# Merging the two strip tasks of V into one task of the scheduler

## The chip, the cores and the metric

The kernel runs on one core of a Trainium2 chip. The metric is the device time of one execution in microseconds (us). Times are medians of several runs; a ratio is the mean time of one kernel's fast runs over the mean of the other's in the same rounds, so it is not quite the ratio of the medians quoted beside it. The kernel before has a median of 1903.02 us (1902.42 to 1903.92, three runs).

## The reference, cut to what matters

Two layers A alternate with two feed-forward layers B. Layer A walks over the sequence in 64 segments of 32 rows; 8 rows of memory, made from the attention output of one segment, go into the next. So the steps form a chain.

```python
def _A_ref(x, mem0, Wq, Wk, Wv, Wo, seg_len):      # Wq, Wk, Wv: 512 x 32 heads x 128
    mem = mem0
    for s in range(n_seg):                         # 64 segments
        h = jnp.concatenate([mem, x[:, s*seg_len:(s+1)*seg_len, :]], axis=1)     # 40 rows
        q, k, v = (jnp.einsum('btd,dhe->bhte', h, W) for W in (Wq, Wk, Wv))
        scores = jnp.where(mask, jnp.einsum('bhqe,bhke->bhqk', q, k) * scale, -1e9)
        o = jnp.einsum('bhqk,bhke->bhqe', softmax(scores), v)
        o = jnp.einsum('bhte,hed->btd', o, Wo)
        mem = o[:, :M, :]                          # feeds the next segment
        outs.append(o[:, M:, :])
# x = x + A(layernorm(x)); x = x + B(layernorm(x)); and both once more
```

The four layers are pipelined: step t computes segment t of the first layer A and segment t - 6 of the second, 70 steps in all, with layers B as filler.

## The kernel before

The kernel is recorded as tasks. A planner (a list scheduler with 24 rounds, made in Python before anything runs) gives each task an engine, a place in that engine's order, and its buffers. A task on TensorE is never interrupted, but two tasks can be separated by any other that is more urgent. L568 and the like are lines of the kernel. PSUM is the memory into which the kernel's matmuls write, in the eight banks of its pool `bank`; the tiles `qku`, `ptsb`, `otsb` and `sst` hold copies out of it.

```python
class Kern:
    ...
        self.bank = Pool([... 8 PSUM banks ...], {"bg": 3, "v": 3})
    ...
    def emit_step(self, t):
        ...
        vb = [pl.buf(self.bank), pl.buf(self.bank)]

        def strips(q):
            for c in range(DC):                    # 4 chunks of the contraction
                for i in range(4):                 # 4 strips of 32 partitions
                    k = 2 * i + q
                    nc.tensor.matmul(vb[q][32 * i:32 * i + 32, :], lhsT=hT[:, c, SCOL:SCOL + 32], rhs=self.wv[:, c, k * 512:(k + 1) * 512],
                                     start=(c == 0), stop=(c == DC - 1), skip_group_check=True)

        def add_strips():
            sb = pl.buf(self.sstp)
            for q in range(2):
                pl.add("PE", DC * (mm_ns(512) + 12) + 75, lambda q=q: strips(q), r=hkeys + [("wv", h) for h in range(H)], w=[vb[q]], use=[sb])
            for q in range(2):
                pl.add(("ACT", "DVE"), copy_ns(512), lambda q=q: (sb[:, q, :], vb[q][:, :]), r=[vb[q]], w=[(sb, q)], use=[sb])
            for i in range(4):
                vu = (4 * t + i) % 5
                pl.add("SP", 430, ...)             # transfer of sb into rows 32 to 63 of the V tile
        ...                                        # q and k (L704), scores (L718), softmax, transposes (L777)
                                                   # P V (L788), output projection (L805)
```

The V rows of the x part are computed in advance for whole blocks (L568). The 32 rows that hold the fresh memory can be computed only in the step itself: these are the strips. A strip matmul has only 32 output partitions, and four run side by side: in the trace of the kernel before they start 2 to 4 ns apart, and the next four 206 ns later in the median. 2 x 16 matmuls fill two PSUM banks. A visit to the strips, below, is a run of strip matmuls with nothing else of TensorE between them. By mode is meant here the output's width: 32 partitions in a strip, and 40, 80 or 128 in the matmuls next to the strips. A switch is the step in TensorE's order from the one to the other. The copies into `sst` and the transfer into the V tile `vsb` follow; P V waits for that tile.

## Time and profile before

| | before |
|---|---|
| median of the timed runs | 1903.02 us |
| profiled run | 1906.87 us |
| TensorE busy | 1853.5 us, 97% |
| waits of TensorE, summed over its view | 44.3 us |
| visits to the strips in TensorE's order | 113 (27 of 32 matmuls, 86 of 16) |
| strip copies on ScalarE and VectorE | 131 and 9 |

How to read it: TensorE is nearly always busy, so what counts is how it spends its busy time. The end that the profile gives for a matmul is modelled, and can lie after the next one's start (904.60 + 1.05 = 905.65 against 905.58 in the prediction's second timeline); the start of the next group less the start of this one, the slot, is what a group really takes of the engine. The prediction below shows the lines. Waits are idle times of more than 0.15 us. The profiled run was 3.9 us slower than the median. The granted clock, used further below, is the share of TensorE's full clock that the chip let it have, as the profile records it (0.992 in the profiled run before).

### The profile page before, as it was taken

What the parts mean: (1) busy time and instruction counts of PE and PEld (TensorE: products, weight loads), DVE (VectorE), ACT (ScalarE), POOL (GpSimd) and SP (SyncE); (2) the same over time, 40 slices, a digit from 0 to 9 for tenths busy, and PEclk for the clock granted to TensorE, in tenths of its full rate; (3) what the DMA queues carried; (4) which work ended last, traced back from release to release, by engine and by line L of the source; (5) the groups of instructions that cost most, each with busy time, mean ns of one, the idle gap of its engine ahead of it and who ended that gap; (6) DMA issues with size and microseconds to landing.
All of it is one profiled execution on the core that took longest, in us unless ns stands there. A gap on an engine that the chain in (4) does not pass through costs nothing.

```text
span 1905.1 us, 94394 instructions
## 1 busy us (share of the span) xinstructions
PE 1853.5 (97%) x41250; PEld 1579.6 (83%) x41250; DVE 1284.5 (67%) x4214; ACT 1192.4 (63%) x2722; POOL 580.1 (30%) x824
## 2 busy tenths in 40 slices
PE   7999899999999999989999999999999999999998
PEld 3578788988988888979888888988888898988786
DVE  5456577776777667756766777767776677766664
ACT  5655567666666666656665666666666666666554
POOL 5412012332424142332413232232413232333311
PEclk9999999999999999999999999999999999999999
DMA  9733324554635454544635454464635444454534
GB/s 350 243 92 106 86 61 141 149 155 118 185 106 165 116 168 127 155 138 128 179 84 172 120 155 140 128 178 134 174 97 167 128 137 141 134 161 138 161 94 139
DMA packets 133965, 273.84 MB, mean 144 GB/s; under 512 B 29254, under 2 KB 65358, under 8 KB 133550
## 3 DMA queue, kind: packets, MB, share of 16 engines
q0 software_dynamic: 59104, 181.61, 32.7%
q1 hardware_dynamic: 74446, 86.19, 15.7%
q8 instruction: 323, 5.29, 1.2%
q14 instruction: 92, 0.75, 0.1%
HBM read 222.04 MB, written 27.26 MB: 131 GB/s over the span
## 4 chain that ended last, share of the span: by engine, by line
PE 87%; DMA 4%; DVE 4%; issue 2%; ACT 2%; SPq 1%; POOL 1%; ACTq 0%; POOLq 0%; DVEq 0%
PE bank L704 30%; PE bank L805 15%; PE bank L904 10%; PE bank L568 8%; PE bank L674 6%; PE bank L928 5%; PE bank L718 5%; PE bank L788 4%; PE bank L777 3%; DMA vsb<-sst 2%; PE bank L538 1%; DMA scr<-vst 1%; DMA xo<-in_A_x_dram 1%; SPq L685 1%; DVE st L731 0%
## 5 line engine op out<-in xcount | busy, mean ns | idle before, releaser
L704 PE MATMUL bank<-hT,wq_sb 128*128 128x80 bf16 (+1 forms) x8960 | 624.8, 198 | 2.8 <-DVE hT L823 0.8
L704 PE MATMUL bank<-hT,wk_sb 128*128 128x80 bf16 (+1 forms) x8960 | 623.4, 198 | 0.4 <-issue 0.4
L996 ACT CAST qku<-bank 128x480 bf16<-128x480 f32 (+3 forms) x770 | 394.6, 512 | 259.3 <-PE bank L704 233.4
L704 PEld LDWEIGHTS <-wq_sb 128*128 128x128 bf16 x8960 | 458.5, 99 | 30.0 <-issue 10.0
L704 PEld LDWEIGHTS <-wk_sb 128*128 128x128 bf16 x8960 | 451.2, 99 | 1.3 <-issue 1.3
L731 DVE TENSOR_TENSOR st<-bank,maskb 80x240 f32<-80x240 f32 (+1 forms) x732 | 269.5, 369 | 196.0 <-PE bank L718 187.3
L805 PE MATMUL bank<-otsb,wo_sb 128*128 128x80 bf16 (+1 forms) x8960 | 375.7, 199 | 3.5 <-ACT otsb L996 2.7
L805 PEld LDWEIGHTS <-wo_sb 128*128 128x128 bf16 x8960 | 341.9, 100 | 14.2 <-issue 4.6
L896 POOL DMA_DIRECT2D wg<-in_B_w_gate_dram x217 | 164.4, 757 | 479.4 <-PE bank L904 430.1
L996 ACT CAST otsb<-bank 128x480 bf16<-128x480 f32 (+3 forms) x420 | 198.7, 486 | 106.2 <-PE bank L788 75.1
L922 POOL DMA_DIRECT2D wd<-in_B_w_down_dram x217 | 154.0, 711 | 221.1 <-PE bank L928 171.2
L526 POOL TENSOR_TENSOR lns<-lns,negh 128x1 f32<-128x1 f32 (+1 forms) x79 | 49.0, 621 | 531.0 <-DVE lns L525 430.1
L760 DVE TENSOR_TENSOR pb<-st,rz 80x480 bf16<-80x480 f32 x348 | 206.0, 593 | 4.4
L743 DVE TENSOR_REDUCE sm<-st 80x6 f32<-80x240 f32 (+3 forms) x420 | 152.8, 364 | 71.7 <-ACT st L741 69.6
L741 ACT ACTIVATE st<-st 80x240 f32<-80x240 f32 (+3 forms) x420 | 159.9, 381 | 27.5 <-DVE st L738 24.5
L718 PE MATMUL bank<-qku 128*80 128x80 bf16 (+1 forms) x2240 | 173.6, 203 | 1.3 <-ACT qku L996 0.3
L718 PEld LDWEIGHTS <-qku 128*80 128x80 bf16 (+1 forms) x2240 | 128.3, 117 | 55.4 <-ACT qku L996 17.0
L904 PE MATMUL bank<-xnT,wu 128*128 128x128 bf16 (+2 forms) x1784 | 171.3, 218 | 1.3 <-DMA wu<-in_B_w_up_dram 1.3
L904 PE MATMUL bank<-xnT,wg 128*128 128x128 bf16 (+2 forms) x1784 | 172.1, 219 | 0.0
L996 ACT CAST ptsb<-bank 128x480 bf16<-128x480 f32 (+3 forms) x277 | 134.5, 495 | 50.9 <-PE bank L777 46.8
L788 PE MATMUL bank<-ptsb,vsb 128*128 128x80 bf16 (+1 forms) x2240 | 141.7, 199 | 24.2 <-DMA vsb<-sst 10.4
L897 POOL DMA_DIRECT2D wu<-in_B_w_up_dram x217 | 163.0, 751 | 5.3 <-PE bank L904 1.6
(103 smaller groups left out, 2578.0 us busy)
## 6 DMA issues: line engine op xcount, KB each, us to landing
wg<-in_B_w_gate_dram POOLq DMA_DIRECT2D x219, 256.0 KB, 4.3
wd<-in_B_w_down_dram POOLq DMA_DIRECT2D x219, 256.0 KB, 4.8
wu<-in_B_w_up_dram POOLq DMA_DIRECT2D x218, 256.0 KB, 4.9
vsb<-scr SPq DMA_DIRECT2D x512, 48.0 KB
vsb<-sst SPq DMA_DIRECT2D x280, 64.0 KB
scr<-vst SPq DMA_DIRECT2D x128, 96.0 KB
wv_sb<-in_A_Wv_dram SPq DMA_DIRECT2D x4, 1024.0 KB
wq_sb<-in_A_Wq_dram SPq DMA_DIRECT2D x5, 768.0 KB
```

The source lines that it names most:

```text
L704: nc.tensor.matmul(o_ap, lhsT=W[:, c, h * P:(h + 1) * P], rhs=mv(c), start=(c == 0), stop=(c == DC - 1))
L718: nc.tensor.matmul(s_all(SB)[pr, uh - h0 + i, :], lhsT=qku[:, i, 0, 0:ncol], rhs=qku[:, i, 1, 0:ncol], start=True, stop=True)
L731: pl.add("DVE", dve_ns(n, True), lambda gsz=gsz, hs=hs, st=st, SB=SB, pj_=pj_, npj_=npj_, mk=mk, idx=idx: nc.vector.tensor_tensor(out=st[p ...
L741: pl.add("ACT", act_ns(n), lambda hs=hs, st=st: nc.scalar.activation(out=st[pr, hs], in_=st[pr, hs], func=ACTF.Exp, scale=self.scale), r=s ...
L760: nc.vector.tensor_tensor(out=o, in0=st[pr, hs].unsqueeze(1).to_broadcast([npart, 2, gsz, L]), in1=rz[pr, :, 0:gsz].unsqueeze(3).to_broadc ...
L788: nc.tensor.matmul(OB[:, hl * ncol:(hl + 1) * ncol], lhsT=self.vsb[(4 * t + h // 8) % 5][:, (h % 8) * P:(h % 8 + 1) * P], rhs=ptsb[:, hl, ...
L805: nc.tensor.matmul(WB[:, c * ncol:(c + 1) * ncol], lhsT=self.wo[:, h, c * P:(c + 1) * P], rhs=otsb[:, hl, 0:ncol], start=(h == 0 and c == ...
L896: pl.add("POOL", 760, lambda wg=wg, fs=fs: nc.gpsimd.dma_start(out=wg[:], in_=self.wgv[:, :, fs]), r=[("wo", self.H - 1)], w=[gk] + bt, la ...
L897: pl.add("POOL", 760, lambda wu=wu, fs=fs: nc.gpsimd.dma_start(out=wu[:], in_=self.wuv[:, :, fs]), r=[("wo", self.H - 1)], w=[uk] + bt, la ...
L904: nc.tensor.matmul(gu[:, 2 * i + k, 0:n], lhsT=W[:, c, i * P:(i + 1) * P], rhs=xnT[:, c, rw], start=(c == 0), stop=(c == DC - 1))
L922: pl.add("POOL", 760, lambda wd=wd, ip=ip: nc.gpsimd.dma_start(out=wd[:], in_=self.wdv[:, 2 * ip:2 * ip + 2, :]), w=[dk] + (["boot"] if se ...
L996: nc.scalar.copy(out=dst, in_=src)
```

## The change

The intent, as it was described, is one task of eight concurrent streams in place of two tasks of four. The loop over the banks moves into the task. The order of the 32 matmuls in it is as before.

```diff
-        def strips(q):
-            for c in range(DC):
-                for i in range(4):
-                    k = 2 * i + q
-                    nc.tensor.matmul(vb[q][32 * i:32 * i + 32, :], ...)
+        def strips():
+            for q in range(2):
+                for c in range(DC):
+                    for i in range(4):
+                        k = 2 * i + q
+                        nc.tensor.matmul(vb[q][32 * i:32 * i + 32, :], ...)
 
         def add_strips():
             sb = pl.buf(self.sstp)
-            for q in range(2):
-                pl.add("PE", DC * (mm_ns(512) + 12) + 75, lambda q=q: strips(q), r=..., w=[vb[q]], use=[sb])
+            pl.add("PE", 2 * DC * (mm_ns(512) + 12) + 150, strips, r=..., w=vb, use=[sb])
```

More of the change, by code (lines that the diff above doesn't have):

```diff
@@ L668, in emit_step @@
         vb = [pl.buf(self.bank), pl.buf(self.bank)]
-        def strips(q):
-            for c in range(DC):
-                for i in range(4):
-                    k = 2 * i + q
-                    nc.tensor.matmul(vb[q][32 * i:32 * i + 32, :], lhsT=hT[:, c, SCOL:SCOL + 32], rhs=self.wv[:, c, k * 512:(k + 1) * 512],
-                                     start=(c == 0), stop=(c == DC - 1), skip_group_check=True)
+        def strips():
[3 more added lines that the diff above has]
+                        k = 2 * i + q
+                        nc.tensor.matmul(vb[q][32 * i:32 * i + 32, :], lhsT=hT[:, c, SCOL:SCOL + 32], rhs=self.wv[:, c, k * 512:(k + 1) * 512],
+                                         start=(c == 0), stop=(c == DC - 1), skip_group_check=True)
         def add_strips():
             sb = pl.buf(self.sstp)
-            for q in range(2):
-                pl.add("PE", DC * (mm_ns(512) + 12) + 75, lambda q=q: strips(q), r=hkeys + [("wv", h) for h in range(H)], w=[vb[q]], use=[sb])
+            pl.add("PE", 2 * DC * (mm_ns(512) + 12) + 150, strips, r=hkeys + [("wv", h) for h in range(H)], w=vb, use=[sb])
             for q in range(2):
```

## The prediction

> **What bounds the kernel now.** I read the share of busy time first, then the chain that ended last, then what the TensorE waits for, then the order of single groups on it.
>
> ```profile
> span 1905.1 us, 94394 instructions
> PE 1853.5 (97%) x41250; PEld 1579.6 (83%) x41250; DVE 1284.5 (67%) x4214; ACT 1192.4 (63%) x2722; POOL 580.1 (30%) x824
> PE 87%; DMA 4%; DVE 4%; issue 2%; ACT 2%; SPq 1%; POOL 1%; ACTq 0%; POOLq 0%; DVEq 0%
> L674 PE MATMUL bank<-wv_sb,hT 128*32 128x512 bf16 x2240 | 141.6, 381 | 0.0
> ```
>
> TensorE is busy 97% of the span and holds 87% of the chain that ended last; the vector and scalar engines have a third of their time free. So a change counts here by what it does to TensorE's own queue. The strips of V, the subject of the change, are the 2240 matmuls of the last line: 70 steps of 32. They show no idle time before them. Two lines of the wait view tell where TensorE does stand still: 10.4 us for the transfer that carries the strips into the V tile, and 7.7 us for one kind of copy.
>
> ```profile
> PE bank L788 <- DMA vsb<-sst: 10.4, 14, 2.1
> PE bank L788 <- DVE ptsb L998: 7.7, 5, 5.7
> ```
>
> All waits of that list add up to about 44 us, most of them at the start, where loads are outstanding, and at the end. The middle is dense: between 300 and 1800 us the table by stretches gives TensorE 1480.6 us busy of 1500.
>
> But "busy" hides something, because ends of matmuls are modelled. I therefore compare starts: the slot of a group is the next group's start minus its own. Here is TensorE's timeline in two steps, one in which the two strip tasks stand together and one in which they are apart:
>
> ```profile
> 557.31 0.31 PE L704 MATMUL bank<-hT,wk_sb 128*128 128x80 bf16 x4
> 557.55 1.91 PE L674 MATMUL bank<-wv_sb,hT 128*32 128x512 bf16 x32
> 559.39 0.42 PE L718 MATMUL bank<-qku 128*80 128x80 bf16 x6
> ```
>
> ```profile
> 904.16 0.51 PE L718 MATMUL bank<-qku 128*80 128x80 bf16 x9
> 904.60 1.05 PE L674 MATMUL bank<-wv_sb,hT 128*32 128x512 bf16 x16
> 905.58 0.31 PE L718 MATMUL bank<-qku 128*80 128x80 bf16 x3
> 905.82 1.05 PE L674 MATMUL bank<-wv_sb,hT 128*32 128x512 bf16 x16
> 906.79 0.32 PE L704 MATMUL bank<-hT,wq_sb 128*128 128x80 bf16 x4
> ```
>
> Together: 32 matmuls hold the engine 559.39 - 557.55 = 1.84 us. Apart: 0.98 and 0.97, so 1.95 for the same 32. The 16 by themselves should stream four deep in 4 x 0.216 = 0.86, the rate of the ordinary 512-wide matmuls (L568, 8 in 1.72 us): each visit to the strips pays about 0.115 us on leaving. It also pays on entering: four L704 matmuls take 0.143 us each time, but 0.24 ahead of the strips (+0.10); three L718 matmuls take 0.11 elsewhere and 0.24 ahead of the second half (+0.13). Over the whole trace, the median excess is 117 ns in the groups that follow strips out, and 97 (after L704), 113 (after L718) and 99 ns (after L928) in the groups ahead of them.
>
> [...] the changed loop also keeps its two banks one after the other. The trace agrees: 32 strips take 1.84 us, twice 0.86 plus one switch. The array's work does not shrink.
> [...]
>
> **The change part by part.**
>
> It removes no matmul, weight load or byte: TensorE has 41251 matmuls in both built programs, and the loop inside the new task is in the old order (bank, contraction chunk, strip). What changes is that the scheduler can no longer put another task between the two halves. The order of the built programs says how much that is: before, the strips form 113 visits (27 of 32 matmuls, 86 of 16), so 43 of the 70 steps are split, by anything from 3 short matmuls to 140. After, there are 70 visits, all of 32.
>
> So 43 entries and 43 exits go. The entries before stand behind L704 45 times (0.097), L718 43 times (0.113), L928 20 times (0.099): about 0.105 each. Sum: 43 x (0.105 + 0.117) = **9.5 us**. Check by the pair of steps above: apart 1.95 + 0.13 for the second entry against 1.84, which is 0.24 a step. All of it lies on TensorE, in the dense middle of the kernel, so nearly all of it should be on the path: 9.5 us or 0.5% of 1903.
>
> What moves: the copies out of the banks become due together. Before, ScalarE does 131 of the 140 and VectorE 9; in the changed order 82 and 58. Some ptsb copies go the other way (ScalarE 277 to 295), so VectorE gains 13 instructions net: 13 x 0.69 (its strip copy) = 9 us on an engine with over 600 us free. Nothing on the path.
>
> What it adds: each task needs both banks at once and holds the first one some 0.9 us longer, and a score matmul (L718) that comes due just after the strips began waits up to 1.84 us instead of 0.98. In the split steps the second half now comes earlier. From the order, weighing each matmul by its streaming time and each switch by 0.11 us, I estimate the work on TensorE between the last strip and the first use of the V tile: under 6 us in 66 of 70 steps before, in 53 after. The transfer behind the 10.4 us of waits thus has a little more room.
>
> **The rivals.**
>
> *New waits eat the gain.* All other tasks are rescheduled as well. For: strips were filler that fitted into short gaps (8 of the splits are by just 3 score matmuls, which feed the softmax chain); a block of 1.84 us delays those. Against: TensorE always has other filler in the middle, and 1480.6 of 1500 us is already dense. If each of the 43 steps lost 0.2 us, the time would stay at 1903; if the start and the end fall badly, some 1908.
>
> *Fewer waits for the V tile.* The earlier second halves could save up to the 10.4 us of waits for its transfer; half of it would give 1888. For: the 66 to 53 above. Against: 14 waits in 70 steps come from the transfer's own latency and from reschedules alike, and steps with under 5 us of room remain.
>
> *The scalar or vector engine becomes the bound.* At 63% and 67% with 13 instructions moved, I see nothing for this; time unchanged by it.
>
> *The switch cost is hidden anyway.* If TensorE waited after the strips in any case, the switches would cost nothing. Against: idle before the strips is 0.0, and the following groups start at once. Then 1903.
>
> **Range and chances.** 1903.0 - 9.5 = 1893.5. Waits could move either way; a redone schedule of this size may shift them by some 5 us (a tenth of the 44 us, one 5.7 us wait more or less). I lean slightly to a partial loss and take **1894.5 us**, with 1885.5 to 1904 for 8 in 10. Two per cent are 38 us: faster than that would need all of the waits to vanish as well, slower would need a wait of 0.5 us in every step. Faster 0.01, within 2% 0.98, slower 0.01.
>
> **What would show it.** In the timeline after, strips come only as x32 with slots of 1.84; the excess at switches falls by 9 to 10 us; busy TensorE falls by about as much, and its waits stay near 44 us. ScalarE's sst copies fall to 82. I am wrong if the waits of TensorE (for vsb, for ptsb, for banks) grow by over 9 us, or if the x32 groups cost more than 1.84[...].

The prediction does not say where its streaming times come from; the median slots in the trace before are 36 ns at 80 columns (L704), 56 at 128 (L904) and 216 at 512 (L568). The room before the first use of the V tile, under 6 us in 66 and in 53 steps, is an estimate that was not measured. What the trace before shows of the transfer: in the 14 waits for it, P V starts 3.6 to 6.8 us after the second strip copy has ended (median 4.8).

## The result, and the profile after

The changed kernel takes 1896.05 us (median of four runs, 1893.69 to 1900.82), against 1903.01 for the kernel before beside it: 7.0 us less. The ratio is 0.9966, with a 95% interval of 0.9946 to 0.9986. That is the same within 2%, but clearly faster.

| | before | after |
|---|---|---|
| median of the timed runs | 1903.01 us | 1896.05 us |
| profiled run | 1906.87 us | 1895.58 us |
| TensorE busy | 1853.5 us | 1842.5 us |
| waits of TensorE, summed | 44.3 us | 44.9 us |
| visits to the strips | 113 | 70 |
| strip copies on ScalarE and VectorE | 131 and 9 | 82 and 58 |

The first lines of the page after:

```profile
span 1893.8 us, 94493 instructions
PE 1842.5 (97%) x41250; PEld 1582.0 (84%) x41250; DVE 1288.9 (68%) x4227; ACT 1178.3 (62%) x2709; POOL 581.2 (31%) x826
PE 88%; DMA 4%; ACT 3%; issue 2%; DVE 1%; POOL 1%; SPq 0%; POOLq 0%; ACTq 0%; DVEq 0%
```

The number of matmuls is the same, 41250, but TensorE is busy 11.0 us less (not all of it by the switches; the part on the prediction takes it apart). The shares have not moved: the same engine bounds the kernel. This is a step in TensorE's timeline after (start, duration, engine, line, operation, names, shape and count), to be held against the split step that the prediction shows:

```profile
256.72 0.51 PE L718 MATMUL bank<-qku 128*80 128x80 bf16 x9
257.17 1.91 PE L675 MATMUL bank<-wv_sb,hT 128*32 128x512 bf16 x32
259.00 0.31 PE L718 MATMUL bank<-qku 128*80 128x80 bf16 x3
```

Nine score matmuls still hold the engine 0.45 us, where nine at 38 ns (the median slot of L718) would hold it 0.34, so the entry is still paid; then 32 strip matmuls hold it 1.83 us. In the split step the same 32 took 0.98 + 0.97, and the three score matmuls between them 0.24 instead of 0.11. Four of the five longest waits of TensorE after, without the 7.8 us at the start that both kernels have (line, what it waited for, total us, times, longest):

```profile
PE bank L788 <- DMA vsb<-sst: 8.5, 13, 2.0
PE bank L704 <- DVE hT L818: 6.1, 6, 3.9
PE bank L538 <- ACT xn L529: 5.8, 5, 3.4
PE bank L805 <- ACT otsb L996: 5.3, 16, 0.7
```

The waits are other ones, but their sum is the same. The waits for the strip transfer are 8.5 us instead of 10.4.

### The profile page after: what moved, and what is told of

The parts are those of the page before. It is cut to its first block, busy times and chain, and to the rows that moved or that the text cites. A ratio compares the mean times of both kernels' runs of the same rounds, so it can differ in the third digit from the quotient of the medians.

```text
span 1893.8 us, 94493 instructions
## 1 busy us (share of the span) xinstructions
PE 1842.5 (97%) x41250; PEld 1582.0 (84%) x41250; DVE 1288.9 (68%) x4227; ACT 1178.3 (62%) x2709; POOL 581.2 (31%) x826
## 4 chain that ended last, share of the span: by engine, by line
PE 88%; DMA 4%; ACT 3%; issue 2%; DVE 1%; POOL 1%; SPq 0%; POOLq 0%; ACTq 0%; DVEq 0%
PE bank L704 31%; PE bank L805 15%; PE bank L904 10%; PE bank L568 9%; PE bank L675 7%; PE bank L928 5%; PE bank L718 5%; PE bank L788 4%; PE bank L777 3%; DMA vsb<-sst 2%; PE bank L538 1%; ACT otsb L996 1%; ACT ptsb L996 1%; DMA wu<-in_B_w_up_dram 1%; ACT qku L996 0%
## 5 line engine op out<-in xcount | busy, mean ns | idle before, releaser
L704 PE MATMUL bank<-hT,wq_sb 128*128 128x80 bf16 (+1 forms) x8960 | 626.2, 198 | 9.0 <-DVE hT L818 6.1
L704 PE MATMUL bank<-hT,wk_sb 128*128 128x80 bf16 (+1 forms) x8960 | 624.9, 198 | 0.3 <-issue 0.3
L704 PEld LDWEIGHTS <-wq_sb 128*128 128x128 bf16 x8960 | 459.0, 99 | 38.1 <-issue 15.6
L704 PEld LDWEIGHTS <-wk_sb 128*128 128x128 bf16 x8960 | 451.6, 99 | 0.4 <-issue 0.4
L526 POOL TENSOR_TENSOR lns<-lns,negh 128x1 f32<-128x1 f32 (+1 forms) x79 | 47.8, 606 | 569.4 <-DVE lns L525 354.7
L718 PE MATMUL bank<-qku 128*80 128x80 bf16 (+1 forms) x2240 | 178.2, 202 | 1.0 <-ACT qku L996 0.9
L904 PE MATMUL bank<-xnT,wg 128*128 128x128 bf16 (+2 forms) x1784 | 172.1, 219 | 1.3 <-ACT xnT L996 1.2
L996 ACT CAST ptsb<-bank 128x480 bf16<-128x480 f32 (+3 forms) x295 | 145.2, 501 | 43.2 <-PE bank L777 40.5
L904 PE MATMUL bank<-xnT,wu 128*128 128x128 bf16 (+2 forms) x1784 | 171.5, 219 | 0.4 <-DMA wu<-in_B_w_up_dram 0.3
L718 PEld LDWEIGHTS <-qku 128*80 128x80 bf16 (+1 forms) x2240 | 131.1, 117 | 44.0 <-issue 19.5
L738 DVE TENSOR_TENSOR st<-st,mx 80x240 f32<-80x240 f32 (+3 forms) x420 | 156.0, 371 | 4.1
```

Source lines behind the costliest of these rows:

```text
L704: nc.tensor.matmul(o_ap, lhsT=W[:, c, h * P:(h + 1) * P], rhs=mv(c), start=(c == 0), stop=(c == DC - 1))
L718: nc.tensor.matmul(s_all(SB)[pr, uh - h0 + i, :], lhsT=qku[:, i, 0, 0:ncol], rhs=qku[:, i, 1, 0:ncol], start=True, stop=True)
L738: pl.add("DVE", dve_ns(n), lambda gsz=gsz, hs=hs, st=st, mx=mx: nc.vector.tensor_tensor(out=st[pr, hs], in0=st[pr, hs], in1=mx[pr, hs].uns ...
L904: nc.tensor.matmul(gu[:, 2 * i + k, 0:n], lhsT=W[:, c, i * P:(i + 1) * P], rhs=xnT[:, c, rw], start=(c == 0), stop=(c == DC - 1))
L996: nc.scalar.copy(out=dst, in_=src)
```

## The experiments

The theory is that each visit to the strips costs a switch on the way in and one on the way out, 0.105 + 0.117 = 0.22 us in the trace before, and that the change gains by making 43 visits less. The rivals are: eight streams overlap better than four; the switch costs nothing on the path; holding a bank longer takes part of the gain back; the gain is luck of a schedule that was redone as a whole. There were twelve runs in three sets. Each set had its own chip and its own runs of the kernel before, whose mean was 1905.8, 1904.5 and 1908.6 us. So ratios or differences within a set are compared, not times across sets. All results were correct.

### One switch more in each step

The switch itself is put back, and nothing else. Apart from the 70 added matmuls with their weight loads, the instructions stand in the changed kernel's order on every engine.

```diff
             for q in range(2):
+                if q:
+                    nc.tensor.matmul(vb[1][:, 0:32], lhsT=self.ident[:, :], rhs=hT[:, 0, 0:32], start=True, stop=True, skip_group_check=True)
                 for c in range(DC):
```

> The changed kernel with one full-width matmul of 32 columns put between the two halves of each strip task[...]; the schedule is otherwise the same, instruction for instruction. If a switch in and out costs 0.222 us on the path: 70 x (0.222 + about 0.03 for the matmul itself) = 17 to 18 us over the changed kernel, some 1914 us; slot of a step's strips 2.09 instead of 1.84. If switches are hidden behind other waits: under 1900 us.

Median 1915.87 us, ratio to the kernel before 1.0052 (1.0039 to 1.0066). The changed kernel has 0.9966, so the added switches cost 0.0086 of 1903, some 16.4 us. Its timeline:

```profile
582.30 0.28 PE L720 MATMUL bank<-qku 128*80 128x80 bf16 x3
582.50 1.05 PE L677 MATMUL bank<-wv_sb,hT 128*32 128x512 bf16 x16
583.48 0.19 PE L673 MATMUL bank<-hT,ident 128*128 128x32 bf16 x1
583.60 1.05 PE L677 MATMUL bank<-wv_sb,hT 128*32 128x512 bf16 x16
584.58 0.31 PE L720 MATMUL bank<-qku 128*80 128x80 bf16 x3
```

A half takes 0.98 us again, and one matmul of 32 columns holds the engine 0.12. The whole is 2.08 us, 0.24 more than 1.84; 70 x 0.24 = 16.8 us. The interleaved kernel below, of the same set and with the changed kernel's order of groups, has a mean of 1899.6 us against 1915.8 here: 16.2 us. So the slots account for the measured time, to within the intervals of some 4 to 5 us, and the switch lies on the path.

### The same matmul in the strips' own mode

The control: the same place, but the output has 32 partitions.

```diff
+                if q:
+                    nc.tensor.matmul(vb[1][0:32, 0:32], lhsT=self.ident[:, 0:32], rhs=hT[:, 0, 0:32], start=True, stop=True, skip_group_check=True)
```

> The control for the run before: the added matmul writes 32 partitions, in the same mode as the strips. If it is the change of mode that costs: 70 x about 0.03 = 2 us over the changed kernel, some 1898 us, slot about 1.87. If any interruption of the strips costs the same: some 1914 us, like the full-width one.

```profile
582.32 0.28 PE L720 MATMUL bank<-qku 128*80 128x80 bf16 x3
582.52 1.05 PE L677 MATMUL bank<-wv_sb,hT 128*32 128x512 bf16 x16
583.40 0.18 PE L673 MATMUL bank<-hT,ident 128*32 128x32 bf16 x1
583.40 1.05 PE L677 MATMUL bank<-wv_sb,hT 128*32 128x512 bf16 x16
584.38 0.31 PE L720 MATMUL bank<-qku 128*80 128x80 bf16 x3
```

On TensorE this is what was expected: 1.86 us for the whole, 0.02 more than without, and no gap at the added matmul. It is the other width that costs (0.24 us for the full-width matmul, 0.02 for this one), not the interruption. The first half holds the engine 0.88 us here (583.40 - 582.52), as no switch follows it, and 0.98 with one.

The weight loads (PEld) show more. First the load of the added full-width matmul, then that of the control:

```profile
583.48 0.10 PEld L673 LDWEIGHTS <-ident 128*128 128x128 bf16 x1 [0.42 <-issue]
```

```profile
583.18 0.10 PEld L673 LDWEIGHTS <-ident 128*32 128x32 bf16 x1
```

Both loads take 0.10 us. The first starts only with its matmul (583.48), the second 0.22 us ahead of it (583.40). The changed kernel's own profile has the same pattern: a load starts 2 ns ahead of its matmul at the 70 entries and 70 exits, 34 ns ahead elsewhere and 214 ns ahead between strips (medians). The cost of a switch, 0.10 to 0.12 us, is about the length of one load, 0.10. What takes this time is not shown.

But the time did not follow: 1906.74 us (1898.76 to 1910.99), ratio 1.0000 (0.9981 to 1.0019), some 6.5 us over the changed kernel, where 2 were expected. I ran it again beside the changed kernel on another chip.

> The same-mode control again, since it came out some 6 us above the changed kernel where 2 were expected, with a slot only 0.02 us longer. If that excess was scatter of the waits of that chip's runs: within 3 us of the changed kernel of this same set. If it is a real cost of the added matmul: 5 to 8 us above it again.

> The changed kernel once more, with more rounds and beside the next runs on one chip. Expected: 0.9966 of the kernel before within its interval (0.9946 to 0.9986), that is 4 to 9 us faster.

The second time it had 0.9982 (0.9964 to 0.9999) and the changed kernel 0.9968 (0.9951 to 0.9986): by their means of 1905.17 and 1902.64, a difference of 2.5 us, within the 3 us. So most of the first excess did not repeat. What is left over 70 x 0.02 = 1.4 us is within the scatter. By time alone, the control of the first set lies 9.9 us below the run with the switch (means 1905.9 and 1915.8), where the slots give 70 x 0.22 = 15.4; it is the slots that show the switch as the cause, and the times support it in part. TensorE's waits in the profiles were 52.4 us the first time and 48.3 the second, and 47.3 in the changed kernel's second profile; why the first set had more stays open.

### Eight accumulations side by side

```diff
-            for q in range(2):
-                for c in range(DC):
+            for c in range(DC):
+                for q in range(2):
                     for i in range(4):
```

> The changed kernel with the loop over banks inside the loop over chunks, so that eight accumulations are really open side by side. Theory[...]: no change, slots 1.84 us, time within 3 us of the changed kernel. Rival (eight streams overlap more than four): slots fall below 1.7 us, and the time by 70 x 0.14 = 10 us, to 1886.

The ratio is 0.9967 (0.9954 to 0.9981), that of the changed kernel. The slot has not moved:

```profile
340.31 0.31 PE L704 MATMUL bank<-hT,wk_sb 128*128 128x80 bf16 x4
340.55 1.91 PE L675 MATMUL bank<-wv_sb,hT 128*32 128x512 bf16 x32
342.39 0.42 PE L718 MATMUL bank<-qku 128*80 128x80 bf16 x6
```

340.55 to 342.39 is 1.84 us. More open accumulations give no more overlap (1.84 us in either order); the eight concurrent streams are not the reason for the gain.

### An early copy of the first bank

In the changed kernel the copies of both banks start after the whole task. Here the planner may start the first one after the first half.

```diff
-                    n.ready = max(n.ready, end + self.gap(tk, n))
+                    n.ready = max(n.ready, end + self.gap(tk, n) - n.lead)
...
+                if q == 0:                         # the copy of the first bank
+                    tk.lead = DC * (mm_ns(512) + 12) + 75
```

> The changed kernel, but the scheduler lets the first bank's copy start when the first half of the task is done (0.985 us earlier), so that bank comes free early as it did before. Theory (only the switches count): still 70 visits, within 4 us of the changed kernel, 1892 to 1900. Rival (the late copy and the longer hold of a bank took back part of the gain): 2 to 6 us faster than the changed kernel, 1890 to 1894.

The profile shows the copy starting 1.10 us after the strips (558.11 after 557.01), as it did in the adjacent steps of the kernel before, and ScalarE doing 134 of the 140 copies again. The ratio is 0.9960 (0.9945 to 0.9974). Against 0.9966 and 0.9968 that is 1 us or so, inside the intervals: holding the bank longer costs nothing that these runs can resolve. The edit also made a new plan (12 of its visits follow L928, against 3), so even this 1 us can't be put down to the copy. The expected times named for the rival were for another chip; by ratio it would have needed 0.9955 or less, and the interval still reaches there (0.9945), so a cost of 2 to 4 us is not excluded.

### Replanned kernels: how much is luck?

The planner may order tasks anew everywhere when one duration changes. So both kernels were planned anew with a strip duration that differs by 4 ns a half. The edit is the number 75 changed to 79 or 71 (in the changed kernel 150 to 158 or 142). These kernels have 114 and 121 visits, and 70 and 70.

> The kernel before, replanned: only the duration that the scheduler assumes for a strip task is 4 ns longer. 114 visits to the strips in its order against 113. Theory (visits at 0.222 us decide): 1903 us within 3. Rival (the gain of the change was luck of the replanning): as far from 1903 as the changed kernel is, 7 us either way.

> The kernel before, replanned with 4 ns less for a strip task: 121 visits. Theory: 8 more visits x 0.222 = 1.8 us over 1903, so 1905 within 3. Rival (replanning noise): anywhere in 1896 to 1910.

> The changed kernel, replanned with 8 ns more for the merged strip task: 70 visits. Theory: 1896 within 3, below both replans of the kernel before by 43 to 51 visits x 0.222 = 9.5 to 11 us. Rival (noise): the two families overlap.

> The changed kernel, replanned with 8 ns less for the merged strip task: 70 visits. Theory: 1896 within 3. Rival (noise): overlaps with the replans of the kernel before.

| kernel | visits | mean us | ratio (95% interval) | waits of TensorE in its profile |
|---|---|---|---|---|
| before | 113 | 1904.5 | 1 | 44.3 us |
| before, +4 ns | 114 | 1911.5 | 1.0036 (1.0014 to 1.0057) | 50.5 us |
| before, -4 ns | 121 | 1911.2 | 1.0033 (1.0014 to 1.0052) | 50.6 us |
| after, +8 ns | 70 | 1897.2 | 0.9961 (0.9945 to 0.9977) | 46.1 us |
| after, -8 ns | 70 | 1898.5 | 0.9968 (0.9950 to 0.9985) | 47.8 us |

The result was not the expected one for the kernel before: both replans are 7 us slower, although one visit more should cost 0.2 us and eight 1.8. Its schedule was a fortunate one. What made it so is not shown. The replans' profiles (one each) have 6 us more waits, but all four profiles of this set lack 212 to 226 of the 41250 matmul records (their weight loads are complete), and such a hole can count as a wait: `PE bank L568 <- issue: 2.5, 14, 0.5` stands in one of them, and no line of L568 with `issue` in any profile with complete records. Waits for which the trace names no releaser (`issue`) sum to 9.3 and 3.5 us in the two replans and 1.1 in the kernel before; without them the waits are 41.2, 47.1 and 43.2 us. The changed kernel's replans lie within 1.3 us of each other and keep its ratio. The families do not overlap, not even by single runs of the set. The mean of the three schedules of before is 1909.0, that of the two replans of after 1897.9: 11.1 us apart. Visits alone give (116 - 70) x 0.222 = 10.2 us. That the two are so near proves little, since the granted clock differs too (see the end); that a switch costs time was shown by putting it back. But as far as three schedules of each kind can tell, with 0.9966 and 0.9968 for the changed kernel's own, the gain is not the luck of one schedule: the luck was on the side of the kernel before, and made the gain look smaller.

Two waits that differ, in the two kernels of -4 and -8 ns (other lines between them left out); first the one with split strips:

```profile
PE bank L788 <- DMA vsb<-sst: 14.7, 19, 2.3
PE bank L777 <- DVE pb L760: 5.9, 1, 5.9
```

```profile
PE bank L788 <- DMA vsb<-sst: 6.1, 10, 2.6
PE bank L704 <- DVE hT L818: 5.7, 5, 4.4
```

TensorE waits for the strip transfer 10.4, 8.9 and 14.7 us in the three schedules with split strips (before, +4, -4), and 8.5, 5.0 and 6.1 with merged ones (after, +8, -8). That is some 5 us in the mean. The room that the earlier second half gives would explain it, but no run tests this alone, and two profiles of the changed kernel itself differ by 1.8 us (8.5 and 6.7).

### A stall that both kernels have

The second line of each pair above has one long wait in it (5.9 and 4.4 us). All profiles up to here have it near 810 us, 3.9 to 6.2 us long, under different names. The chain of waits of the kernel before names it (start, us, what):

```profile
805.38 0.61 DVE xo L937
806.00 0.02 issue
806.02 4.09 DMA out_dram<-xo
810.11 0.02 issue
810.13 5.58 DMA xo<-in_A_x_dram
815.71 0.02 issue
815.73 0.69 DVE lns L523
```

The output block is written from a buffer, and only then is a block of x loaded into the same buffer; VectorE stands idle for 6.22 us before the layernorm (L523, at 815.73) that needs it; the ptsb copy for which TensorE waits 5.68 us comes behind it, at 816.34. The edit gives these loads the other buffer.

```diff
-            i = self.nxt("xp", 2)
-            xb, key = self.xp[i], (("xo", 0) if i == 0 else "xp1")
+            xb, key = self.xp[1], "xp1"
```

> The changed kernel with the late x blocks loaded into their own buffer, never into the one from which the output is written. All profiles so far show TensorE waiting 3.9 to 6.2 us near 810 us; the chain there is the output write of 4 us, then the load of 4 to 6 us into the same buffer. If that chain makes the stall: the wait near 810 us is gone, with it the dip of the granted clock (1.7 us), and the time falls by 4 to 7 us, to about 1890. If another wait stands behind it: no change.

> The kernel before with that same buffer edit: strips in 107 visits. If the two effects are independent: 37 visits x 0.222 = 8 us slower than the changed kernel with the edit, that is some 1898, and 4 to 7 us faster than the replans of the kernel before (1910). If the edit takes over the gain: the two are within 3 us.

In the set with the changed kernel (0.9968), the changed kernel with the edit has 0.9946 (0.9928 to 0.9965), 1897.91 us against 1902.29 (by the means 4.2 us less). Its table by stretches near 810 us (stretch, its length, busy time with instructions of TensorE, weight loads, VectorE, ScalarE and GpSimd, granted clock, share and rate of the transfers), under that of the changed kernel:

```profile
800.00:810.00 10.00, 8.19 (x170) 7.36 (x167) 4.48 (x17) 4.35 (x10) 3.66 (x6) 1.00 0.87 253
810.00:820.00 10.00, 7.89 (x169) 7.89 (x169) 5.09 (x18) 4.79 (x12) 4.12 (x6) 0.83 0.37 108
```

```profile
800.00:810.00 10.00, 10.00 (x230) 9.48 (x227) 8.08 (x31) 6.92 (x17) 6.58 (x9) 1.00 0.70 201
810.00:820.00 10.00, 10.00 (x238) 9.10 (x239) 4.92 (x14) 5.30 (x13) 5.35 (x8) 1.00 0.74 210
```

TensorE is busy throughout, and the clock's dip to 0.83 is gone. This is the fastest version that ran; it beats both kernels. The kernel before with the edit has 107 visits and 1905.56 us, ratio 0.9977 (0.9955 to 0.9999), by the means 6.6 us more than the changed kernel with it; 37 visits x 0.222 = 8.2 were expected. So the two gains add up here, as far as can be told: both edits also made new plans, which alone can move a kernel by several us. The absolute times expected were too low, since this chip ran all kernels slower.

## Why the prediction was right or wrong

The time of 1896.05 us lies in the range, 1.5 us above the point, and within 2% as forecast.

- **The size of a switch: right.** 43 switches less should give 9.5 us. Slots in the trace: 27 x 1.84 + 86 x 0.98 = 134.0 us before and 70 x 1.84 = 128.8 after, that is 5.2 us on leaving; the excess of the groups ahead of the strips, summed over the visits without those that wait, falls from 11.8 to 7.1 us. Together 9.9. The kernel with the switch put back confirms the size in another way.
- **The switch is on the path: right.** 16.4 us measured for 16.8 us of slots, and 16.2 within one set.
- **No x32 slot over 1.84: right but for exceptions.** One of the 70 visits, at 181 us, had a slot of 3.06: after its first seven matmuls there is a gap for which the trace shows no wait (0.84 us by the wait view), and this is no switch.
- **Busy falls as much, waits stay near 44 us: right in number, by some luck.** Busy fell 11.0 us; waits are 44.9. But the granted clock, which the prediction left out, was 0.992 in the profiled run before and 0.996 in that after: nine stretches of 3.41 us at half clock against four. Counted from the traces, TensorE's slots in these stretches exceed the same slots elsewhere by some 11 us before and 5 after. So some 6 us of the 11.0 come from the clock and 9 to 10 from the switches, while short delays between other groups, each under 0.15 us, grew by some 4. The two profiled runs differ by 11.3 us, the medians by 7.0.
- **Strip copies on ScalarE fall to 82: right,** and VectorE has 58.
- **Eight streams are no gain: right,** shown by the interleaved kernel (1.84 us a slot, as in the changed kernel).
- **New waits eat the gain: not seen.** Of 9.5 us, 7.0 arrived, but the interval of the ratio runs from 2.7 to 10.3 us, so this run alone shows no loss. The waits of the pair grew by only 0.6 us. What the prediction's sum left out is the luck of a single schedule: both replans of the kernel before are 7 us slower than it, and between families the gain is 11.1 us.
- **Fewer waits for the V tile: right in direction.** 10.4 to 8.5 us in this pair, some 5 us in the mean of the families; its cause was argued, not tested.
- **A scalar or vector engine as the bound: nothing of it is seen.** They are at 62% and 68%.
- **Two asides of the prediction are off.** From 1893.5 us, 2% faster than before would need 28.5 of the 44 us of waits, not all; 2% slower would need 47.5 us, 0.7 us a step and not 0.5. Neither bears on the result.

What stays open: what made the old schedule fortunate, how much each of its waits is worth in time, and what share the clock has. Within a kernel, the runs with a lower mean granted clock are the longer ones (about 1.3 us for each 0.001, over 104 runs of the three sets), and the kernels with split strips had a mean clock of 0.990 to 0.993 in those sets, the others 0.994 to 0.996. By that slope the clock goes with some 2 us of the 6 to 7 us that the changed kernel and its replans gain within their sets, and with 3 of the 11.1 us between families. Most dips follow a wait of TensorE: in the pair's two profiles 10 of the 11 within the span begin during a wait of over 0.15 us or at most 2.2 us after one (that at 816 us in the kernel before in a wait of 5.7). So part of this is the same effect seen twice; it was not separated.

## What to carry to other kernels

If small matmuls run side by side as these strips do, put all that are due in one place: in this kernel, whose TensorE is busy 97% of the span, every visit cost 0.22 us, whether 16 or 32 matmuls came with it. A scheduler that counts this cost as part of the task's length can't see that it belongs to the visit, so it splits for free; tie the tasks together. And before a gain of half a per cent is believed or given up, replan both kernels with a trifling difference: here that alone moved the old one by 7 us.

## What the traces show of the switch, the matmuls of 512 columns and the clock

- A switch: 0.10 to 0.11 us on entering and 0.115 us on leaving; 0.24 us for one full-width matmul of 32 columns put between strips, against 0.02 us for one in the strips' mode; weight loads start 2 ns ahead of their matmul at a switch, 34 ns elsewhere and 214 ns between strips.
- Matmuls of 512 columns and full width, one after another (L568): eight hold the engine 1.73 us (967.84 to 969.57 in the kernel before), 216 ns each.
- The clock: in the kernel before, a wait of 1.82 us (971.8 to 973.6), the only one over 0.15 us in the 10 us before it ends, goes with a clock at half from 973.3 on, for some 3.4 us (twice what the granted shares below lack of 1: 0.34 + 0.50 + 0.50 + 0.36). The table by stretches shows it; the last three columns are granted clock, share and rate of the transfers:

```profile
972.00:973.00 1.00, 0.00 (x0) 0.00 (x0) 0.19 (x2) 0.19 (x1) 0.00 (x0) 1.00 0.36 90
973.00:974.00 1.00, 0.37 (x7) 0.40 (x8) 0.00 (x0) 0.00 (x0) 0.00 (x0) 0.66 0.31 74
974.00:975.00 1.00, 1.00 (x16) 0.79 (x14) 0.70 (x3) 0.77 (x2) 0.00 (x0) 0.50 0.64 163
975.00:976.00 1.00, 1.00 (x18) 1.00 (x17) 1.00 (x9) 0.26 (x1) 0.55 (x1) 0.50 0.58 144
976.00:977.00 1.00, 1.00 (x23) 1.00 (x21) 0.62 (x2) 0.12 (x1) 0.00 (x0) 0.64 0.06 21
977.00:978.00 1.00, 1.00 (x34) 1.00 (x31) 0.33 (x2) 1.00 (x3) 0.00 (x0) 1.00 0.17 47
```

